# Gate logits of a fused attention, feed-forward and top-1 expert kernel: token columns moving past weights held in four column groups, in place of weights moving past tokens

## The chip, the cores and the metric

The kernel runs on one core of a Trainium2 chip. The metric is the device time of one execution in microseconds (us). Engines are named as in the profile: PE (TensorE, matmul; PEld are its weight loads), DVE (VectorE), ACT (ScalarE), POOL (GpSimd) and SP (SyncE, which issues most DMAs).

## The reference

Three layers run one after another on 1536 tokens (2 batches of 768) of width 512: attention with a local band and a few global keys, a SiLU feed-forward layer of width 2048, and a layer of 8 experts of which each token uses one. The change touches the gates of the last.

```
def _moe2_ref(x, w_gate, w_output_gate, w1, w2):
    logits = x @ w_gate                                  # 1536 x 8
    e_idx = np.argmax(logits, axis=1)
    probs = softmax of logits; gate_w = probs[np.arange(N), e_idx]
    eom = 1.0 / (1.0 + np.exp(-(x @ w_output_gate)))     # 1536 x 8
    for e in range(8):
        mask = e_idx == e
        h = np.maximum(x[mask] @ w1[e], 0.0)             # 512 -> 1024
        out[mask] = gate_w[mask, None] * eom[mask, e, None] * (h @ w2[e])
```

(The two lines on the softmax are shortened here.) The 8 columns of `w_gate` and the 8 of `w_output_gate` stand side by side, so each token needs 16 sums over 512 numbers. An expert must be chosen exactly, so these products are made in float32.

## The kernel before

The tokens are 12 tiles of 128 rows (`n` = 0 to 11), taken in six pairs (`u` = 0 to 5). Attention for the first batch comes first. Then comes the feed-forward stage, a loop over steps `g` (from L966): five groups of pairs, `CH` = [0,1], [2], [3], [4], [5], each with 16 steps `f` over slices of the width 2048. Attention for the second batch is woven into its first four groups.

In each step PE gets, in this order: `s1_mm` (L319, 12 matmuls, x times a slice of `w_in`), two score products of attention where a slot of attention falls in the step (`qkp`, L151), the products with V (`pv`, L224), now and then four transposes (`ms`, L241), then whatever `run_gates` takes from the list `gq`, and last `s2_mm` (L339 to L341, 6 matmuls with `w_out`, of the step two before). On ACT and DVE stand `s1_ev` (tanh on ACT L323, product on DVE L324) and `s1_sp` (ACT L327, DVE L328), which must end before that `s2_mm`'s data two steps later; they are issued ahead of `run_gates` in the same step, so each engine does them first. All engines work through their own instructions strictly in the order written (`manual_schedule`).

The list `gq` sets where the gates go. When a group of pairs is finished, one entry is put on it for each piece of each pair: `s2_ev` (the layer's result to SBUF), two `gate1` (four transposes on PE to a PSUM bank, ACT copies them to `xtf`, so that x stands with its 512 numbers on partitions, 4 blocks of 128), then `gate2`, `gate3`, `gate4`; a step takes one entry from the list, or two at two places that L987 names by number. `gate2` issues `logits` for both tiles and then seven DVE operations (L394 to L400): the maximum, the chosen expert as a one-hot row `eb`, and the running count `esum`. `gate3` begins on PE with six small products `gr` (L406 to L408) that need `eb` and `esum`, and goes on with DVE (L410 to L422) to the row number at which each token is scattered (L429) for its expert. The pair `u`=4 ends one group before the last, so its gates fall into steps of the last group, where no attention is left. The gates of the last pair, `u`=5, are called by hand in `moe2` (L660), between pieces of the first expert's work (`early1`, `late1`).

`logits(n)`, L379, is what the change rewrites: a block of x (128 x 128) is stationary, the 16 columns of `wgs` move, and four such products accumulate to 128 token rows x 16:

```
for k in range(KC): T.matmul(glp[n//2][:,n%2],x[:,k,:],wgs[:,k,:],start=(k==0),stop=(k==KC-1))
```

PSUM banks for these small tiles (`qkp`, `ms`, `gt`, `gl`, `gr`) come from `abank` (L113), which hands out the tags of `atags` in turn; in the stretch where the gates run there are three. A tile that is given a bank waits until everything issued on the tile that had it before has been done.

Of the kernel before, what the change touches and what calls it, by code (L numbers as in the profile page):

```python
# [10 lines left out]
F32 = mybir.dt.float32  # L11
# [5 lines left out]
AF = mybir.ActivationFunctionType  # L17
ALU = mybir.AluOpType
AX = mybir.AxisListType
P = 128  # L20
# [3 lines left out]
def kernel(ctx, tc, qk, v, n_global, n_local, w_in, w_out, wg, w1, w2, out):  # L24
# [38 lines left out]
    vpr=vpr4.bitcast(BF16).rearrange("p z (m d) -> p z m d",m=3)  # L63
    NWI=FB+FB//2
    woh={}
    wgs=const.tile([P,KC,16],F32,name="wgs")
    upper=const.tile([P,P],BF16,name="upper"); ones=const.tile([P,P],BF16,name="ones")
    c3=const.tile([P,8],BF16,name="c3"); rev=const.tile([P,8],F32,name="rev"); tok=const.tile([P,NTT],I32,name="tok")
    esum=const.tile([P,NTT+1,8],BF16,name="esum")
# [43 lines left out]
    def abank(shape,name):  # L113
        tg=atags[0][acnt[0]%len(atags[0])]; acnt[0]+=1
        return ps.tile(shape,F32,tag=tg,name=name,bufs=1)
# [235 lines left out]
    def gate_consts():  # L351
        G.memset(ones,1.0)
        G.memset(upper,1.0)
        G.affine_select(out=upper,in_=upper,pattern=[[1,P]],compare_op=ALU.is_gt,fill=0.0,base=0,channel_multiplier=-1)
        G.memset(esum,0.0)
        G.iota(tok,pattern=[[P,NTT]],base=0,channel_multiplier=1)
        it=mp.tile([P,2,8],I32,tag="gsm",name="it",bufs=2)
        G.iota(it[:,0],pattern=[[-1,8]],base=8,channel_multiplier=0)
        G.tensor_copy(rev,it[:,0])
        G.iota(it[:,1],pattern=[[CAP//P,8]],base=0,channel_multiplier=0)  # L360
        G.tensor_copy(c3,it[:,1])
        for p,w in enumerate(WIN): G.memset(capk[:,p:p+1],8.0*w+8)
        S.dma_start(wgs,wg.rearrange("(k p) e -> p k e",p=P))
    zr=[]
    def rows_init():
        z=mp.tile([P,XW],F32,tag="xT",name="zr",bufs=3); zr.append(z)
# [9 lines left out]
        A.activation(out=x,in_=m,func=AF.Copy)  # L376
    gsm={}
    glp={}
    def logits(n):  # L379
        if n%2==0: glp[n//2]=abank([P,2,16],"gl")  # L380
        x=xts.pop(n)
        for k in range(KC): T.matmul(glp[n//2][:,n%2],x[:,k,:],wgs[:,k,:],start=(k==0),stop=(k==KC-1))  # L382
    def gate2(u):

        for n in (2*u,2*u+1):
            if n in xts: logits(n)
        g=glp.pop(u)
        lg=g[:,:,0:8]
        s=mp.tile([P,2,32],F32,tag="gsm",name="gsm",bufs=2)
        eb=mp.tile([P,2,8],BF16,tag="geb",name="geb",bufs=2)  # L390
        gsm[u]=s,eb
        w=s[:,:,0:8]; mxl=s[:,:,24:25]; mxr=s[:,:,25:26]
        b8=lambda x: x.to_broadcast([P,2,8])
        V.tensor_reduce(out=mxl[:,:,0],in_=lg,axis=AX.X,op=ALU.max)  # L394
        V.tensor_tensor(out=w,in0=lg,in1=b8(mxl),op=ALU.subtract)
        V.scalar_tensor_tensor(out=s[:,:,8:16],in0=w,scalar=0.0,in1=rev[:,None,:].to_broadcast([P,2,8]),op0=ALU.is_equal,op1=ALU.mult)
        V.tensor_reduce(out=mxr[:,:,0],in_=s[:,:,8:16],axis=AX.X,op=ALU.max)
        V.tensor_tensor(out=eb,in0=s[:,:,8:16],in1=b8(mxr),op=ALU.is_equal)
        for t in range(2): V.tensor_tensor(out=esum[:,2*u+t+1],in0=esum[:,2*u+t],in1=eb[:,t],op=ALU.add)
        V.tensor_tensor(out=s[:,:,16:24],in0=g[:,:,8:16],in1=eb,op=ALU.mult)  # L400
# [26 lines left out]
    def gate4(u,t):  # L427
        di,xr=gdi[u]
        G.indirect_dma_start(out=XE[:,:],out_offset=bass.IndirectOffsetOnAxis(ap=di[:,t:t+1],axis=0),in_=xr[:,t,:],in_offset=None,bounds_check=NE*CAP-1,oob_is_err=False)  # L429
# [230 lines left out]
    def moe2():  # L660
        late_split()
        early1(0,0)
        run_gates(2)
        early1(0,1)
        logits(NTT-2)
        early1(1,0)
        run_gates(1)
        late1()
        run_gates(1)
        early1(1,1)  # L670
        run_gates(1)
        early2(0)
        late3()
        order(1)
        moe2_open2()
        load_x(1); load_t(0)
        early3(0,0)
        early2(1)
        early3(0,1); early3(1,0)
        early3(1,1)  # L680
        early4()
        atags[0]=['a','pv','s23']
        LG=2
        steps=[(p,f) for p in range(NE) for f in range(8)]
        for g in range(len(steps)+LG):
            if g<len(steps):
                p,f=steps[g]
                def spl():
                    split_u(4*(p+1)+nq[1]//4,nq[1]%4,nq[1]%4==1); nq[1]+=1
                f1_mm(p,f)  # L690
                if p+1<NE and f==0: nq[:]=[0,0]
                if g==4: flags()
                ns=(0,0,3,3,3,3,2,2)[f] if p+1<NE else 0
                f1_ev(p,f,spl if ns else lambda: None)
                if p+1<NE:
                    for _ in range(ns-1): spl()
                    while nq[0]<min(16,nq[1]+4*(f+1),nq[1]+NQR): load_u(4*(p+1)+nq[0]//4,nq[0]%4); nq[0]+=1
                    if p and f==0: load_x(p+1)
                    if p==0 and f==5:
                        for k,(j,n) in enumerate(tiles(0)): tail(0,j,xwt[0][:,k,0:1],xwt[0][:,k,1:2])  # L700
                    t=tiles(p+1)
                    px=PX
                    if px<=f<px+len(t): prep_x(p+1,t[f-px][0])
            if g>=LG:
                p2,f2=steps[g-LG]
                if p2<NE-1:
                    f2_mm(p2,f2)
                    if f2==7: f2_ev(p2)
                elif f2<LASTF:
                    f2_mm(p2,f2)  # L710
                elif f2==7:
                    for r in tiles(p2):
                        for k in range(LASTF,8): f2_mm(p2,k,[r])
                        f2_ev(p2,[r])
# [225 lines left out]
    with tc.manual_schedule():  # L940
        params()
        want(2); load_v(0)
        table_ints()
        V.tensor_copy(pf,pi)
        table(slice(3,4))
        tab_heads(slice(3,4),slice(3,4),range(H))
        rows_init()
        s=0
        while s<SB:
            for k,e in enumerate(slot_b(s)):  # L950
                e()
                if k==0 and s>=DQ: dec_op()
            if s%2==0 and 4<=s<4+2*NE: rows_clear(s//2-2)
            s+=1
            for x in WP.get(s,()): w_to(*x)
        atags[0]=['s20','s21','s22','s23']
        gate_consts()

        steps=[(c,f) for c in range(len(CH)) for f in range(FB)]
        pend=[]  # L960
        gq=[]
        def run_ev(k):
            for _ in range(min(k,len(pend))): pend.pop(0)()
        def run_gates(k):
            for _ in range(min(k,len(gq))): gq.pop(0)()
        for g in range(len(steps)+LAG):  # L966
            live=g<len(steps)
            if live:
                c,f=steps[g]
                if c==0:  # L970
                    w_to(0,0,g+LI); w_to(0,1,g+(LO if g<LS else 1)); w_to(2,0,f+1)
                for u in CH[c]: s1_mm(u,f)
                for u in CH[c]: s1_ev(u,f)
                if c==0:
                    for _ in range(2):
                        if s<SB+4: pend+=slot_b(s); s+=1
                    if g==3: atags[0]=['a']
                    if f==FB-1: s=SB
                elif c<4 and s<NS+4 and (f>1 and f!=8 if c==1 else f%2==0):
                    pend+=slot(s); s+=1  # L980
                run_ev(2 if c==0 else 1)
                for u in CH[c]: s1_sp(u,f)
                run_ev(4 if c==0 else 3 if c==1 else 3 if f%2 else 0)
                if g<=FB:
                    w_to(1,0,g+2); w_to(2,1,g-1); w_to(1,1,g)
                if g==FB: load_v(SB//4)
                if g>=LAG+FB: run_gates(2 if g-(len(CH)-1)*FB in (2,4) else 1)  # L987
            if g>=LAG:
                c2,f2=steps[g-LAG]
                s2_mm(c2,f2)  # L990
                if f2==FB-1:
                    for u in CH[c2]: gq.append(lambda u=u: s2_ev(u))
                    if c2==0: gq.append(lambda: atags.__setitem__(0,['a','s22','s23']))
                    for u in CH[c2]:
                        for n in (2*u,2*u+1): gq.append(lambda n=n: gate1(n))
                        for fn in (gate2,gate3,lambda u: gate4(u,1)): gq.append(lambda u=u,fn=fn: fn(u))
                    run_gates(3 if c2==0 else 1)
                    if c2==len(CH)-2: gq.append(lambda: order(0))
                    if c2==len(CH)-2: gq.append(moe2_open)
            if live and c>0:  # L1000
                if f==0: load_wol(c,0); load_wol(c,1)
                if f+2<FB: load_wol(c,f+2)
            if g>=len(steps)-FB: moe2_pre(g-len(steps)+FB)
        moe2()
# [43 lines left out]
```

## Time and profile before

| | us |
|---|---|
| median of 3 runs | 621.5 |
| lowest and highest | 619.34 and 621.65 |
| the profiled execution | 621.69 |
| its span, first to last instruction | 620.0 |
| PE busy (4054 matmuls) | 590.6, 95% |
| PE weight loads busy | 500.6, 81% |
| DVE busy | 389.1, 63% |
| ACT busy | 303.0, 49% |
| POOL busy | 186.2, 30% |

The profiled execution is 0.2 above the median of the runs, and 1.7 of it lie outside the span. A busy PE in this table is one that has at least one matmul in flight; matmuls overlap, so what a group of them costs is read from the start of its first to the start of the next group, not from durations. A float32 matmul shows as two records, so the eight matmuls of a pair's logits are 16.

### The profile page before, as it was taken

Reading aid. Unit: us, or ns where it says so; the run is one execution under the profiler, and the core shown is the slowest. Engines: PE = TensorE matmul, PEld = TensorE weight load, DVE = VectorE, ACT = ScalarE, POOL = GpSimd, SP = SyncE. Lnnn points to the kernel's source line nnn. Section 1 sums busy time; section 2 is a strip of 40 time slices with the busy share of each in tenths; the row PEclk is TensorE's granted clock in tenths of the full one; section 3 lists DMA queues with packets and bytes.
Section 4 is the critical chain, followed back from the end, with each engine's and each line's share of the span. In section 5 each row is a group of like instructions: output and inputs, shape, how many; then the busy total and the mean of one; then the engine's idle time right before and its main releaser. Section 6 shows DMA issues by size and latency. Waiting matters only on the chain.

```text
span 620.0 us, 12009 instructions
## 1 busy us (share of the span) xinstructions
PE 590.6 (95%) x4054; PEld 500.6 (81%) x4054; DVE 389.1 (63%) x1069; ACT 303.0 (49%) x802; POOL 186.2 (30%) x233
## 2 busy tenths in 40 slices
PE   2999899999999999999999999999899999999996
PEld 1566788888888888888889999888788888888884
DVE  4388669999737764756463345744844678778840
ACT  5377634334353445343532234644653666776641
POOL 3367614444314252131221001112231432331321
PEclk9999999999999999999999999999999999999999
DMA  7639725674355587465444327607845378569500
GB/s 255 243 79 355 218 89 159 215 221 158 116 160 148 149 192 170 106 177 130 115 89 141 86 84 259 254 19 246 263 162 185 127 259 269 184 212 290 162 17 21
DMA packets 81511, 105.18 MB, mean 170 GB/s; under 512 B 29978, under 2 KB 44314, under 8 KB 81441
## 3 DMA queue, kind: packets, MB, share of 16 engines
q1 hardware_dynamic: 75712, 94.79, 50.4%
q0 software_dynamic: 2288, 6.39, 2.8%
q10 hardware_dynamic: 3440, 3.15, 1.6%
q8 instruction: 34, 0.56, 0.4%
q14 instruction: 37, 0.30, 0.2%
HBM read 81.46 MB, written 17.99 MB: 160 GB/s over the span
## 4 chain that ended last, share of the span: by engine, by line
PE 69%; issue 8%; DVE 8%; DMA 6%; ACT 4%; POOL 3%; SPq 1%; ACTq 0%; POOLq 0%; DVEq 0%
PE s L319 17%; PE s L339 6%; PE s L340 5%; PE s L341 5%; PE h L616 5%; PE h L622 4%; PE qkp L151 4%; PE y L639 4%; PE y L641 4%; PE y L640 4%; PE tp L194 3%; PE h L617 2%; POOL wol L303 2%; PE pv L224 2%; PE gl L382 1%
## 5 line engine op out<-in xcount | busy, mean ns | idle before, releaser
L319 PEld LDWEIGHTS s<-xT,wi 128*128 128x128 f32 x1152 | 147.3, 190 | 13.1 <-DVE g L328 6.0
L319 PE MATMUL s<-xT,wi 128*128 128x256 f32 x1152 | 152.2, 284 | 1.9 <-DVE xT L248 1.4
L323 ACT ACTIVATE u<-s 128x256 f32<-128x256 f32 x96 | 35.3, 381 | 112.3 <-PE s L319 111.5
L324 DVE SCALAR_TENSOR_TENSOR s<-u,s 128x256 f32<-128x256 f32 x96 | 39.8, 427 | 79.4 <-ACT u L323 79.4
L339 PE MATMUL s<-woh,g 128*128 128x512 f32 x192 | 79.2, 413 | 0.0
L491 DVE TENSOR_TENSOR uq<-qr,uq 128x512 fp32r<-128x512 f32 x87 | 71.2, 841 | 7.2 <-ACT uq L490 4.4
L340 PE MATMUL s<-woh,g 128*128 128x512 f32 x192 | 75.5, 393 | 0.0
L490 ACT ACTIVATE uq<-qr 128x512 fp32r<-128x512 f32 x112 | 66.4, 626 | 4.4 <-DMA qr<-in_w_dram 4.1
L328 DVE TENSOR_TENSOR g<-s,g 128x256 fp32r<-128x256 f32 x96 | 39.3, 422 | 31.7 <-ACT g L327 27.3
L327 ACT ACTIVATE g<-s 128x256 fp32r<-128x256 f32 x96 | 35.7, 380 | 40.3 <-DVE s L324 40.3
L639 PE MATMUL y<-uq,hh 128*128 128x512 f32 (+6 forms) x136 | 55.2, 406 | 0.0
L641 PE MATMUL y<-uq,hh 128*128 128x512 f32 (+6 forms) x136 | 53.6, 394 | 0.0
L640 PE MATMUL y<-uq,hh 128*128 128x512 f32 (+6 forms) x136 | 53.4, 393 | 0.0
L491 POOL TENSOR_TENSOR uq<-qr,uq 128x512 fp32r<-128x512 f32 x25 | 32.9, 1326 | 62.1 <-ACT uq L490 62.1
L151 PE MATMUL qkp<-ring 64*128 64x256 f32 (+1 forms) x192 | 36.0, 455 | 14.3 <-DMA ring<-in_qk_dram 13.4
L170 ACT ACTIVATE t<-t,mx 128x256 f32<-128x256 f32 (+1 forms) x96 | 45.8, 480 | 6.5 <-DVE mx L163 4.6
L631 ACT ACTIVATE hh<-h 128x224 fp32r<-128x224 f32 (+6 forms) x64 | 23.3, 364 | 47.3 <-DVE h L629 27.3
L632 DVE SCALAR_TENSOR_TENSOR hh<-h,hh 128x224 fp32r<-128x224 f32 (+6 forms) x64 | 25.3, 395 | 31.8 <-ACT hh L631 31.8
L339 PEld LDWEIGHTS s<-woh,g 128*128 128x128 f32 x192 | 36.3, 189 | 7.1 <-ACT u L323 2.0
L340 PEld LDWEIGHTS s<-woh,g 128*128 128x128 f32 x192 | 36.3, 189 | 5.0
L577 POOL DMA_INDIRECT out_dram<-y,ixt x17 | 17.4, 1024 | 74.9 <-ACT y L646 56.7
L341 PE MATMUL s<-wolr,g 128*128 128x512 f32 x128 | 39.6, 390 | 0.0
(215 smaller groups left out, 1071.7 us busy)
## 6 DMA issues: line engine op xcount, KB each, us to landing
qr<-in_w_dram SPq DMA_DIRECT2D x128, 256.0 KB
wolr<-wlo_d SPq DMA_DIRECT2D x64, 256.0 KB
wiraw<-in_w_in_dram SPq DMA_DIRECT2D x16, 512.0 KB
wraw<-in_w_out_dram SPq DMA_DIRECT2D x13, 512.0 KB
xe<-zr SPq DMA_DIRECT2D x8, 792.0 KB
wlo_d<-wol SPq DMA_DIRECT2D x16, 256.0 KB
xw<-xe SPq DMA_DIRECT2D x15, 264.0 KB
ring<-in_qk_dram SPq DMA_DIRECT2D x12, 256.0 KB
```

The lines of the kernel that those rows point to most:

```text
L151: T.matmul(q[:,sl],w[:,z,1],w[:,z:z+1,0] if i==0 else w[:,0:3:2,0] if z==0 else w[:,z-1:z+1,0],start=True,stop=True)
L170: A.activation(out=t[:,j,:ce],in_=t[:,j,:ce],func=AF.Exp,scale=0.125,bias=mx[n][:,h:h+1],accum_out=ss[n][:,h:h+1])
L319: T.matmul(t,w[:,ww,kc,:],x[:,xx,kc,:],start=(k==0),stop=(k==11)); k+=1
L324: V.scalar_tensor_tensor(out=t,in0=u,scalar=1.0,in1=t,op0=ALU.add,op1=ALU.mult)
L339: T.matmul(o,g[u][:,0,sl],wh,start=(f==0),stop=False)
L340: T.matmul(o,g[u][:,1,sl],wh,start=False,stop=False)
L341: else: T.matmul(o,g[u][:,0,sl],wl,start=False,stop=(f==FB-1))
L490: A.activation(out=t[:,0],in_=r,func=AF.Copy)
L491: (G if (i%2 if pool is None else pool) else V).tensor_tensor(out=t[:,1],in0=r,in1=t[:,0],op=ALU.subtract)
L639: T.matmul(o,g[:,0,sl],w[:,0],start=(f==0),stop=False)
L640: T.matmul(o,g[:,1,sl],w[:,0],start=False,stop=False)
L641: T.matmul(o,g[:,0,sl],w[:,1],start=False,stop=(f==7))
```

## The change

`logits` is turned round. The 16 weight columns of a block (with the 16 of the next block behind them, so that a group is 32 wide) are now stationary, in column group `k` for block `k`, and the 128 tokens of the block move. The four products don't accumulate: each writes its own 32 partitions of a tile of 128 x 128, of which ACT makes a copy in SBUF (in the place of x's first block). A second product has that copy stationary and a constant `sel` (128 x 16, ones where the row is 32k + column) moving; it adds the four groups and brings tokens back to partitions. This second product stands at the head of `gate2`; the first ones get an entry of their own in the list, `gate2a`, ahead of it. The entry makes the list longer, and a third step (number 5 after the last group's start) takes two entries. In `moe2` both tiles' first products stand together ahead of `early1(1,0)`, and the second behind it. The bank of `gl` now holds a tile from `gate2a` to the end of `gate2`'s DVE operations.

```
-    wgs=const.tile([P,KC,16],F32,name="wgs")
+    wgs=const.tile([P,KC+1,16],F32,name="wgs"); sel=const.tile([P,16],F32,name="sel")
...
-        S.dma_start(wgs,wg.rearrange("(k p) e -> p k e",p=P))
+        S.dma_start(wgs[:,0:KC],wg.rearrange("(k p) e -> p k e",p=P))
+        G.memset(wgs[:,KC],0.0)
+        G.tensor_tensor(out=sel,in0=ident[:,0:16],in1=ident[:,32:48],op=ALU.add)
+        for k in (2,3): G.tensor_tensor(out=sel,in0=sel,in1=ident[:,32*k:32*k+16],op=ALU.add)
...
     def logits(n):
-        if n%2==0: glp[n//2]=abank([P,2,16],"gl")
-        x=xts.pop(n)
-        for k in range(KC): T.matmul(glp[n//2][:,n%2],x[:,k,:],wgs[:,k,:],start=(k==0),stop=(k==KC-1))
-    def gate2(u):
-
+        if n%2==0: glp[n//2]=abank([P,KC,P],"gl")
+        x=xts.pop(n); q=glp[n//2][:,1+n%2]
+        for k in range(KC): T.matmul(q[32*k:32*(k+1),:],wgs[:,k:k+2,:].rearrange("p a e -> p (a e)"),x[:,k,:],start=True,stop=True)
+        A.activation(out=x[:,0,:],in_=q,func=AF.Copy); xls[n]=x
+    def gate2a(u):
         for n in (2*u,2*u+1):
             if n in xts: logits(n)
-        g=glp.pop(u)
+    def gate2(u):
+
+        g=glp.pop(u)[:,0,0:32].rearrange("p (t e) -> p t e",t=2)
+        for t in range(2): T.matmul(g[:,t],xls.pop(2*u+t)[:,0,:],sel,start=True,stop=True)
...
         logits(NTT-2)
+        run_gates(1)
         early1(1,0)
...
-                if g>=LAG+FB: run_gates(2 if g-(len(CH)-1)*FB in (2,4) else 1)
+                if g>=LAG+FB: run_gates(2 if g-(len(CH)-1)*FB in (2,4,5) else 1)
...
-                        for fn in (gate2,gate3,lambda u: gate4(u,1)): gq.append(lambda u=u,fn=fn: fn(u))
+                        for fn in (gate2a,gate2,gate3,lambda u: gate4(u,1)): gq.append(lambda u=u,fn=fn: fn(u))
```

What this moves is seen in the order of the instructions. First PE in the steps 3 and 4 of the last group, where the gates of pair `u`=4 stand; `s` are tiles of the feed-forward layer (12 matmuls of `s1_mm`, 6 of `s2_mm`), `gl` the logits, `gr` the products of `gate3`. Before:

```order
L319 MATMUL s_4580<-xT,wi 128x256 x12
L382 MATMUL gl<-wgs,xtf 128x16 x8
L339 MATMUL s_4570<-woh,g 128x512
L340 MATMUL s_4570<-woh,g 128x512
L339 MATMUL s_4571<-woh,g 128x512
L340 MATMUL s_4571<-woh,g 128x512
L341 MATMUL s_4570<-wolr,g 128x512
L341 MATMUL s_4571<-wolr,g 128x512
L319 MATMUL s_4626<-xT,wi 128x256 x12
L406 LDWEIGHTS upper
L406 MATMUL gr<-geb,upper 128x8
```

Now:

```order
L319 MATMUL s_4601<-xT,wi 128x256 x12
L386 MATMUL gl<-xtf,wgs 32x128 x8
L339 MATMUL s_4591<-woh,g 128x512
L340 MATMUL s_4591<-woh,g 128x512
L339 MATMUL s_4592<-woh,g 128x512
L340 MATMUL s_4592<-woh,g 128x512
L341 MATMUL s_4591<-wolr,g 128x512
L341 MATMUL s_4592<-wolr,g 128x512
L319 MATMUL s_4639<-xT,wi 128x256 x12
L394 MATMUL gl<-sel,xtf 128x16 x2
L413 LDWEIGHTS upper
L413 MATMUL gr<-geb,upper 128x8
```

The logits' last product has come to stand directly ahead of `gr`; between the two there was a whole `s2_mm` and a whole `s1_mm`.

DVE at the same place, before:

```order
L324 SCALAR_TENSOR_TENSOR s_4580<-u,s_4580 128x256
L328 TENSOR_TENSOR g<-s_4580,g 128x256
L394 TENSOR_REDUCE gsm<-gl 128x2
L395 TENSOR_TENSOR gsm<-gl,gsm 128x2x8
L396 SCALAR_TENSOR_TENSOR gsm<-gsm,rev 128x2x8
L397 TENSOR_REDUCE gsm<-gsm 128x2
L398 TENSOR_TENSOR geb<-gsm 128x16
L399 TENSOR_TENSOR esum<-esum,geb 128x8 x2
L400 TENSOR_TENSOR gsm<-gl,geb 128x2x8
L324 SCALAR_TENSOR_TENSOR s_4626<-u,s_4626 128x256
L328 TENSOR_TENSOR g<-s_4626,g 128x256
L410 TENSOR_TENSOR gsm<-gr,geb 128x2x8
```

Now:

```order
L324 SCALAR_TENSOR_TENSOR s_4639<-u,s_4639 128x256
L328 TENSOR_TENSOR g<-s_4639,g 128x256
L401 TENSOR_REDUCE gsm<-gl 128x2
L402 TENSOR_TENSOR gsm<-gl,gsm 128x2x8
L403 SCALAR_TENSOR_TENSOR gsm<-gsm,rev 128x2x8
L404 TENSOR_REDUCE gsm<-gsm 128x2
L405 TENSOR_TENSOR geb<-gsm 128x16
L406 TENSOR_TENSOR esum<-esum,geb 128x8 x2
L407 TENSOR_TENSOR gsm<-gl,geb 128x2x8
L417 TENSOR_TENSOR gsm<-gr,geb 128x2x8
```

`gate2`'s seven operations stand behind `L324` and `L328` of the later step, the one in which PE reaches `gr`.

Last PE for the last pair, in `moe2`; `eh` is the first expert's early product, `ec` the gather of its rows. Before:

```order
L555 MATMUL eh<-qb,exT 128x512 x6
L382 MATMUL gl<-wgs,xtf 128x16 x4
L555 MATMUL eh<-uq,exT 128x512 x6
L382 MATMUL gl<-wgs,xtf 128x16 x4
L536 MATMUL ec_5176<-eI,ehl 128x128 x2
```

Now:

```order
L562 MATMUL eh<-qb,exT 128x512 x6
L386 MATMUL gl<-xtf,wgs 32x128 x8
L562 MATMUL eh<-uq,exT 128x512 x6
L394 MATMUL gl<-sel,xtf 128x16 x2
L543 MATMUL ec_5205<-eI,ehl 128x128 x2
```

The second tile's first products have moved ahead of the six `eh`, and the small product took their place ahead of `ec`.

## Rows read from the trace of the kernel before

**Rows 1.** Busy time by stretch: start:end, length, busy by engine (instructions), clock, DMA

```profile
184.00:403.00 219.00, 218.01 (x1779) 191.36 (x1778) 123.43 (x410) 92.52 (x272) 47.02 (x48) 1.00 0.56 149
425.00:590.00 165.00, 161.23 (x906) 136.74 (x906) 115.88 (x236) 103.43 (x233) 49.29 (x41) 1.00 0.66 217
```

**Rows 2.** Timeline of PE at the first pair's logits: start, length, instruction

```profile
184.51 1.96 PE L382 MATMUL gl<-wgs,xtf 128*128 128x16 f32 x16
186.31 0.48 PE L339 MATMUL s<-woh,g 128*128 128x512 f32 x1
```

**Rows 3.** Timeline at the last pair's second logits and what follows

```profile
407.55 0.60 ACT L558 ACTIVATE ehs<-eh 128x512 f32<-128x512 f32 x1 [0.75 <-PE eh L555]
408.16 1.64 PE L555 MATMUL eh<-uq,exT 128*128 128x512 f32 x6
409.63 0.96 PE L382 MATMUL gl<-wgs,xtf 128*128 128x16 f32 x8
410.44 1.97 PE L536 MATMUL ec<-eI,ehl 128*128 128x128 f32 x16
410.63 0.18 DVE L394 TENSOR_REDUCE gsm<-gl 128x2 f32<-128x16 f32 x1 [3.47 <-PE gl L382]
412.25 0.18 PE L406 MATMUL gr<-geb,upper 128*128 128x8 bf16 x1
```

**Rows 4.** Timeline of PE in attention: products in two column groups, what follows

```profile
61.20 0.66 PE L209 MATMUL px<-pT,vpr 128*64 128x128 f32 x8
61.79 0.70 PE L151 MATMUL qkp<-ring 64*128 64x256 f32 x4
```

**Rows 5.** The same eight, looked at through two narrow windows, 61.66:61.70 and 61.75:61.76

```profile
61.47 0.39 PE L209 MATMUL px<-pT,vpr 128*64 128x128 f32 x4
...
61.58 0.28 PE L209 MATMUL px<-pT,vpr 128*64 128x128 f32 x2
```

**Rows 6.** Instructions of line L209: durations min/median/max in ns, the weight loads

```profile
L209 PEld LDWEIGHTS px<-pT,vpr x176: 132/137/231, 21.3 to 83.6; 128*64 128x64 f32 x176
```

**Rows 7.** Timeline of pair u=4: DVE of gate2, then the step of gate3

```profile
364.71 0.42 DVE L328 TENSOR_TENSOR g<-s,g 128x256 fp32r<-128x256 f32 x1 [0.45 <-ACT g L327]
365.05 0.17 DVE L394 TENSOR_REDUCE gsm<-gl 128x2 f32<-128x16 f32 x1
366.10 0.36 DVE L399 TENSOR_TENSOR esum<-esum,geb 128x8 bf16<-128x8 bf16 x2
366.37 0.17 DVE L400 TENSOR_TENSOR gsm<-gl,geb 128x16 f32<-128x16 f32 x1
367.77 0.18 PE L406 MATMUL gr<-geb,upper 128*128 128x8 bf16 x1
367.93 0.47 PE L339 MATMUL s<-woh,g 128*128 128x512 f32 x1
368.02 0.39 ACT L323 ACTIVATE u<-s 128x256 f32<-128x256 f32 x1 [3.35 <-PE s L319]
369.32 0.42 DVE L328 TENSOR_TENSOR g<-s,g 128x256 fp32r<-128x256 f32 x1 [0.45 <-ACT g L327]
```

**Rows 8.** Timeline of pair u=2: gr, DVE of gate3, the next step's scores

```profile
259.04 0.17 PE L406 MATMUL gr<-geb,upper 128*128 128x8 bf16 x1 [0.26 <-DVE mx L160]
261.38 0.16 DVE L410 TENSOR_TENSOR gsm<-gr,geb 128x16 f32<-128x16 f32 x1
262.18 0.70 PE L151 MATMUL qkp<-ring 64*128 64x256 f32 x4
```

**Rows 9.** Timeline behind gate3 of pair u=1: DVE's last, the next step's scores

```profile
218.43 0.20 DVE L230 RECIPROCAL rs<-rs 128x8 f32<-128x8 f32 x1
219.40 0.30 PEld L151 LDWEIGHTS qkp<-ring 64*128 64x128 f32 x4
```

**Rows 10.** Busy time by stretch at the end, columns as in rows 1

```profile
610.00:615.00 5.00, 3.90 (x17) 2.02 (x15) 0.00 (x0) 1.17 (x2) 1.10 (x2) 1.00 0.17 55
615.00:620.00 5.00, 0.00 (x0) 0.00 (x0) 0.00 (x0) 0.00 (x0) 0.82 (x1) 0.89 0.02 5
```

More of the change, by code (lines that the diff above doesn't have):

```diff
@@ L378 @@
     glp={}
+    xls={}
     def logits(n):
-        if n%2==0: glp[n//2]=abank([P,2,16],"gl")
-        x=xts.pop(n)
-        for k in range(KC): T.matmul(glp[n//2][:,n%2],x[:,k,:],wgs[:,k,:],start=(k==0),stop=(k==KC-1))
-    def gate2(u):
+        if n%2==0: glp[n//2]=abank([P,KC,P],"gl")
[3 more added lines that the diff above has]
+    def gate2a(u):
         for n in (2*u,2*u+1):
             if n in xts: logits(n)
-        g=glp.pop(u)
+    def gate2(u):
+        g=glp.pop(u)[:,0,0:32].rearrange("p (t e) -> p t e",t=2)
+        for t in range(2): T.matmul(g[:,t],xls.pop(2*u+t)[:,0,:],sel,start=True,stop=True)
         lg=g[:,:,0:8]
```

## The prediction, written before the changed kernel ran

> **What bounds the kernel now.** I read the busy time by stretch first. From 184 to 403, where the first five pairs' gates lie, PE is busy for 218.01 of 219.00 us, and in the experts' stage for 161.23 of 165.00 [rows 1]. DVE and ACT stay far below. So PE is the bound on both sides of every place that the change touches, and there a microsecond of PE work saved, or of PE standing still, moves the end by about a microsecond. Then I looked at what the logits cost: not the durations, which overlap, but the start of the group and the start of the next one. At the first pair that is 184.51 to 186.31, 1.80 us for 16 records [rows 2]. Last I followed, for each place of the new order, what PE would wait for there.
>
> **What is removed.** Five pairs at 1.80 make 9.0. At the last pair the two tiles stand apart, 409.63 to 410.44 for one [rows 3], 0.81, so 1.62 for both. Together 10.6 us of PE.
>
> **What is added on PE: the first products.** No row of this trace has four column groups. The nearest is attention's product with V, which writes two halves of the partitions from 64 stationary columns each, with 128 columns moving, as the new logits have. Eight records of it take from 61.20 to 61.79 [rows 4]. Through narrow windows one sees that they start two by two: four are in flight from 61.47 on, the last two from 61.58 [rows 5]. So a round of two costs 0.11, four rounds 0.44, and 0.15 of the 0.59 goes to the change of division, 0.10 of it on leaving (61.58 to 61.79 is a round and 0.10). If all four groups run together, a pair's 16 records are four rounds too, and cost the same 0.59. At three pairs (u=1, 4, 5) full-width work stands directly ahead, where a score product, itself divided, stood or nothing had to change; I add 0.10 each. Sum 6 x 0.59 + 0.3 = 3.8. The bounds: if nothing ran side by side, 16 rounds of 0.11 and the same 0.15, 1.9 a pair; at best four rounds without any price of changing, 0.44. I take the middle value because the row it comes from has the same moving width, the same type and the same change of division.
>
> The same rows bear on a rule that speaks against this change. Two rounds 0.11 apart leave no room for a weight load of 0.137 [rows 5, 6] between them, so loads of one column half run while the other half's product is in flight. The Trainium skill (page "TensorE: Matmul & The Clock Gate", Part 3 on packing small matmuls) says that a weight load overlaps with matmuls in flight only where the row group differs, which column groups don't give; by that a round would be a load and a product. What that would cost is a rival below, and two column halves in this trace don't show it.
>
> **The second product.** Two matmuls, 4 records with a 128-wide stationary side and 16 columns moving, just the form that is removed; at 1.80/16 = 0.11 a record that is 0.45 a pair, 2.7 for six. Added on PE in all 6.5; PE's own work falls by 10.6 - 6.5 = 4.1 us.
>
> **What is added elsewhere.** Twelve ACT copies of 128 x 128. In the steps the second product comes a whole step later, so they are covered. At the last pair the cover is the six `eh` between: ACT is done with `ehs` at 407.55 + 0.60 = 408.15 [rows 3], and the six `eh` there took from 408.16 to 409.63. They now begin a little earlier, about 408.0, and the second product at about 409.3; even at 0.5 each, two copies would be done by then. If that cover were gone, PE would wait for at most those two copies, 1 us. Four small POOL operations at the start stand among other constants, before anything that waits; I cost them at nothing.
>
> **The wait that the change adds.** The third doubled step puts `gate2` and `gate3` of pair u=4 into one step. PE meets the second product and, directly behind, `gr`, which needs `eb` and `esum` from the DVE operations that the second product feeds; and those stand behind `L324` and `L328` of the same step. By the rows: `gr` stood at 367.77 and was over at 367.93; ACT's tanh of that step begins at 368.02 and DVE's `L328` at 369.32 [rows 7]. In the step before, from the start of `L328` at 364.71 to the first of the two additions to `esum` (the pair is 366.10 plus 0.36, so half at 366.28) it is 1.57. So `gr` can't end before 369.32 + 1.57 = 370.9. With only the second product ahead of it it would have ended at 367.93 + 0.45 = 368.4. PE stands still for about **2.6 us**, and `s2_mm` of the step is queued behind. Nothing else can run on PE then, since it works in order, and PE is the bound. What was ahead of `gr` before, a whole `s2_mm` and `s1_mm`, was its cover.
>
> **Bank waits.** The logits' bank is held a step longer, until `L400` (now at the end of the later step's DVE work) has read it, while score products take the three banks in turn. Of pair u=2 the second score product of the step after gets that bank. `gate2` now begins on DVE where `gate3` did, at 261.38 [rows 8], and takes 365.05 to 366.37 + 0.17, 1.49 [rows 7], so the bank is free at 262.9. The scores stood at 262.18; they come 0.45 later for the second product, and 0.16 and 0.26 earlier because `gr` and its wait of 0.26 have left that place [rows 8]: 262.2. A wait of 0.7. At u=1 DVE is free at 218.63 [rows 9], so 220.1 against 219.40 + 0.45 = 219.85: 0.25. At u=0 the same reading gives none, and at u=3 no scores follow in the next step. On the other side the wait of 0.26 at `gr` goes at u=2 and its twin at u=3: 0.5.
>
> **The last pair.** 1.62 goes and 0.69 + 0.45 comes, already in the sum. `L394` would start some 0.5 earlier than 410.63; `gr` waits behind `ec` as before (410.44 to 412.25 against a DVE chain of about 1.5 from 410.63 [rows 3]), so no new wait.
>
> **The sum.** 621.69 - 4.1 + 2.6 + 0.7 + 0.25 - 0.5 = 620.6 for an execution like the profiled one; the median of the runs lies 0.2 under that one, so 620.4 (the rivals below are worked out on the profiled execution). That is 0.2% under 621.5: less than the 0.5% (3.1 us: 618.4 and 624.6) that a measurement of this kernel can tell from no change. What the new products save is given back at one place where two steps of a chain were put together.
>
> **Rivals.**
> - *Two at a time.* If only two column groups run side by side, as the trace shows, a pair needs eight rounds: 4 x 0.11 x 6 = 2.6 more, 623.1. For it: rows 4 show two. Against: nothing in them shows that two is the most. If every round instead had a load of 0.137 ahead of its product, four rounds cost 4 x 0.137 more, 3.3 for six pairs: 623.8. Against that, rows 5. By the rule of the page named above it would be this second figure. Together 0.16; 0.06 of it for the load.
> - *One after another, slower.* If the four products of a tile run one by one, so that the change does not do what its column groups are for, each pair pays 12 more rounds of 0.11, 1.3, at the same place in each step: 7.9, so 628.4. The change comes out slower than before once a pair pays 0.2 more than I take, and by over 0.5% from 0.7. Rows 4 and 5 speak against it. 0.07.
> - *The clock.* PE's clock is 1.00 up to 615 and falls only when PE has long stopped, 0.89 in the last stretch with PE at 0 [rows 10]. If the wait at u=4 took it down to the lower of its two levels, each us there would cost half a us; it takes some 8 us of it to be slower by over 0.5%. 0.03.
> - *The waits are covered, faster.* If `gr`'s wait at u=4 cost nothing, because the step's own chain on ACT and DVE starts sooner than I read or PE catches up later, 617.9. Nothing in rows 1 leaves PE room to catch up. 0.10, with smaller gains elsewhere in it.
>
> **How the numbers follow.** My forecast has 0.64. Its own range is 618.6 to 622.2: the first products at best (1.2 less), of the bank waits (0.9 less if they vanish, 0.9 more if they double), of the wait at u=4 (2.2 to 3.0), beside a spread of the runs that alone is 2.3. The range for 8 in 10 goes on to 623.8, which takes in the first rival. Faster by over 0.5%: 0.12, from the last rival and the low end of the forecast. Slower: 0.13, from one by one, the clock and the upper end of two at a time. Within: 0.75.
>
> **What would show it.** PE from the first record of the new `gl` to the next group: 0.6 to 0.7 for 16 records, where 1.0 would mean two at a time and 1.9 one by one; the records starting in fours. PE idle ahead of `gr` at u=4 for 2.6 us, put down to DVE. Score products at u=2 idle some 0.7 for DVE. `gr` no more waiting at u=2 and 3. PE busy over the whole span some 4 lower, its idle time some 3 higher. If the logits are cheap and the wait at u=4 is not there, I have misread the order; if the wait is there and the time falls by 4 all the same, PE was not the bound that rows 1 make it.

## The result, and the profile after

The changed kernel takes 626.14 us (median of five runs, 624.4 to 628.14) beside 621.13 for the kernel before (five runs). The ratio is 1.0088, with a 95% interval of 1.0061 to 1.0116: slower by 0.9%, outside the range of the prediction. Beside the later experiments it gave 626.41 where before gave 619.26, a ratio of 1.0099 (1.0067 to 1.0132).

The profiled execution took 628.14, and its span is 626.4 with a mean granted clock of 0.990, where before had 0.999. Part 1 of its page, first line (busy us, share of the span, instructions), and then the two stretches of [rows 1] again, columns as there:

```profile
PE 587.5 (94%) x4078; PEld 495.2 (79%) x4078; DVE 386.9 (62%) x1069; ACT 306.2 (49%) x814; POOL 186.8 (30%) x237
```

```profile
184.00:403.00 219.00, 211.16 (x1735) 182.61 (x1735) 115.19 (x392) 87.67 (x263) 42.75 (x45) 0.98 0.54 145
425.00:590.00 165.00, 161.64 (x908) 137.19 (x907) 110.64 (x230) 100.52 (x223) 49.94 (x41) 1.00 0.63 215
```

The experts' stage is as it was (161.23 of 165 before, 161.64 now). In the gates' stretch PE is idle for 7.8 us where it had been idle for 1.0, and the clock there is 0.98; the first pair's first products, at 180.6 to 182.9, now lie ahead of it. PE's busy time over the whole span fell by 3.1 us (590.6 to 587.5); since work at a lower clock counts as longer busy time, this sum alone prices no term.

What PE waits for, from 160 to 432 (line waited at, who ended the wait: us in total, times, longest):

```profile
PE gl L386 <- ACT xtf L387: 5.6, 6, 1.5
PE gr L413 <- DVE geb L405: 2.4, 1, 2.4
PE qkp L151 <- DVE gsm L407: 1.1, 2, 0.8
```

The second line is the wait that the prediction has at 2.6, the third the two bank waits that it has at 0.95 together. The first line is in none of its terms. It is six waits, one a pair, and twice as large as the one that was foreseen.

The first pair shows where it comes from. The timeline of `after` (start, length, engine, line; in brackets the idle time before and who ended it), PE and ACT:

```profile
180.37 0.38 ACT L323 ACTIVATE u<-s 128x256 f32<-128x256 f32 x1 [1.39 <-PE s L319]
...
180.63 0.43 PE L386 MATMUL gl<-xtf,wgs 128*32 128x128 f32 x8
180.65 0.39 ACT L170 ACTIVATE t<-t,mx 128x128 f32<-128x128 f32 x1
...
181.42 0.62 ACT L133 ACTIVATE vpr<-vraw 128x512 bf16<-128x512 f32 x1
...
181.94 0.36 ACT L327 ACTIVATE g<-s 128x256 fp32r<-128x256 f32 x1
...
182.21 0.27 ACT L387 ACTIVATE xtf<-gl 128x128 f32<-128x128 f32 x1
...
182.53 0.43 PE L386 MATMUL gl<-xtf,wgs 128*32 128x128 f32 x8 [1.47 <-ACT xtf L387]
...
182.88 0.50 PE L339 MATMUL s<-woh,g 128*128 128x512 f32 x1
```

The eight records of the first tile are over at 181.06. Those of the second begin at 182.53, just after ACT has finished the copy of the first tile (182.21 + 0.27 = 182.48). That copy is short, but it stands behind everything that the step had already given ACT: `L323`, `L170`, `L133`, `L327`. The order of the program's instructions on PE has the wait written out. Each piece is the place of the first pair; "waits" is the engine whose progress is awaited. In `after`:

```
491 L386 MATMUL gl<-xtf,wgs 32x128 [waits Activation_49]
492 L386 MATMUL gl<-xtf,wgs 32x128 x3
493 L386 MATMUL gl<-xtf,wgs 32x128 [waits Activation_49]
494 L386 MATMUL gl<-xtf,wgs 32x128 x3
```

The first wait is for `xtf` itself, which before had too. The second is new: `logits(n)` issues four products and then the copy, and `gate2a` calls it twice. Both tiles lie in one PSUM tile, in one bank, so the second tile's products are ordered behind ACT's reading of the first. The Trainium skill (page "PSUM — Partial Sum Buffer", section "PSUM bank collisions raise a hardware error") gives the reason for such an order: two engines must not be in the same bank and partitions at once, even at other columns. No run here shows a collision; what the trace shows is the order, 182.53 behind 182.48.

At the other five pairs the same wait is 0.50, 0.96, 0.96, 1.22 and 0.50.

The clock has a part of its own. Busy time by stretch in `after` (columns as in [rows 1], the clock third from the end), around the first pair and around the `gr` of pair u=4:

```profile
180.00:183.50 3.50, 2.03 (x26) 1.22 (x25) 1.96 (x9) 2.38 (x9) 1.16 (x1) 1.00 0.36 63
183.50:187.00 3.50, 3.50 (x15) 3.12 (x14) 0.00 (x0) 0.00 (x0) 0.67 (x1) 0.51 0.42 101
187.00:191.00 4.00, 4.00 (x36) 3.48 (x36) 2.51 (x12) 1.42 (x6) 0.67 (x1) 1.00 0.34 118
...
371.20:378.10 6.90, 6.17 (x26) 5.42 (x27) 2.33 (x15) 0.78 (x3) 1.16 (x2) 0.51 0.25 75
```

Behind the wait of 1.47, and again from the last 0.7 us of the wait of 2.4 at `gr` (which lasted until 371.93), PE runs at the lower of its two levels (0.5, that is 1.2 GHz), though it is busy without a pause for nearly all of the two stretches. 3.5 and 6.9 us at 0.51 do the work of half their length, so about 5 us are lost in this execution, 0.3 of them while PE stood in that wait anyway. The prediction gave this 0.03.

### The profile page after: what moved, and what is told of

The parts are those of the page before. It is cut to its first block, busy times and chain, and to the rows that moved or that the text cites. A ratio compares the mean times of both kernels' runs of the same rounds, so it can differ in the third digit from the quotient of the medians.

```text
span 626.4 us, 12086 instructions
## 1 busy us (share of the span) xinstructions
PE 587.5 (94%) x4078; PEld 495.2 (79%) x4078; DVE 386.9 (62%) x1069; ACT 306.2 (49%) x814; POOL 186.8 (30%) x237
## 4 chain that ended last, share of the span: by engine, by line
PE 63%; DVE 12%; issue 8%; DMA 7%; ACT 6%; POOL 3%; SPq 0%; POOLq 0%; DVEq 0%; ACTq 0%
PE s L319 16%; PE s L339 6%; PE s L340 5%; PE s L341 5%; PE h L623 4%; PE h L629 4%; PE y L646 4%; PE y L648 3%; PE y L647 3%; DMA ring<-in_qk_dram 3%; PE qkp L151 3%; PE tp L194 2%; PE h L624 2%; POOL wol L303 2%; PE pv L224 2%
## 5 line engine op out<-in xcount | busy, mean ns | idle before, releaser
L319 PEld LDWEIGHTS s<-xT,wi 128*128 128x128 f32 x1152 | 149.4, 193 | 13.4 <-DVE g L328 6.0
L319 PE MATMUL s<-xT,wi 128*128 128x256 f32 x1152 | 154.1, 286 | 1.9 <-DVE xT L248 1.4
L324 DVE SCALAR_TENSOR_TENSOR s<-u,s 128x256 f32<-128x256 f32 x96 | 39.7, 426 | 92.2 <-ACT u L323 92.2
L323 ACT ACTIVATE u<-s 128x256 f32<-128x256 f32 x96 | 35.2, 381 | 117.5 <-PE s L319 112.7
L339 PE MATMUL s<-woh,g 128*128 128x512 f32 x192 | 80.4, 419 | 0.0
L498 DVE TENSOR_TENSOR uq<-qr,uq 128x512 fp32r<-128x512 f32 x87 | 74.7, 882 | 7.0 <-ACT uq L497 4.0
L340 PE MATMUL s<-woh,g 128*128 128x512 f32 x192 | 76.3, 397 | 0.0
L328 DVE TENSOR_TENSOR g<-s,g 128x256 fp32r<-128x256 f32 x96 | 39.3, 422 | 30.3 <-ACT g L327 27.1
L327 ACT ACTIVATE g<-s 128x256 fp32r<-128x256 f32 x96 | 35.7, 380 | 39.4 <-DVE s L324 38.9
L170 ACT ACTIVATE t<-t,mx 128x256 f32<-128x256 f32 (+1 forms) x96 | 45.8, 480 | 4.6 <-DVE mx L163 3.8
```

Source lines behind the costliest of these rows:

```text
L170: A.activation(out=t[:,j,:ce],in_=t[:,j,:ce],func=AF.Exp,scale=0.125,bias=mx[n][:,h:h+1],accum_out=ss[n][:,h:h+1])
L319: T.matmul(t,w[:,ww,kc,:],x[:,xx,kc,:],start=(k==0),stop=(k==11)); k+=1
L324: V.scalar_tensor_tensor(out=t,in0=u,scalar=1.0,in1=t,op0=ALU.add,op1=ALU.mult)
L339: T.matmul(o,g[u][:,0,sl],wh,start=(f==0),stop=False)
L340: T.matmul(o,g[u][:,1,sl],wh,start=False,stop=False)
L498: (G if (i%2 if pool is None else pool) else V).tensor_tensor(out=t[:,1],in0=r,in1=t[:,0],op=ALU.subtract)
```

## The experiments

Theory M: the six waits for the copies are the loss, together with the wait at `gr` and the clock that falls behind such waits; the new products themselves cost what was forecast. Its main rival: the products with the array in four column groups cost more than they seem to. R1, R2 and R3 are what the text written ahead of each run calls its rivals; they are not the same in all.

**copies_last: both tiles' products ahead of both copies.**

```
     def logits(n):
...
-        A.activation(out=x[:,0,:],in_=q,func=AF.Copy); xls[n]=x
+        xls[n]=x
     def gate2a(u):
         for n in (2*u,2*u+1):
             if n in xts: logits(n)
+        for t in range(2): A.activation(out=xls[2*u+t][:,0,:],in_=glp[u][:,1+t],func=AF.Copy)
```

> The changed kernel with one thing moved: both tiles' first products are issued before the two ACT copies, so that the second tile's products no longer stand behind the copy of the first. The wait at gr of pair u=4 stays. Theory M (the loss is made of three parts: about 5.6 us at the second tile's products, 2.4 us at gr, and 1 to 5 us in which the clock falls behind these waits): 626.1 - 5.6 and a part of the clock's, 618.5 to 620.5; no PE idle ahead of L386, PE still idle some 2.4 us ahead of gr. Rival R1 (the wait at gr is the cost, and the clock's fall behind it; the second tile's waits lie beside other work): 625 to 626, since gr's wait is untouched.

Measured: 620.18 beside 620.37 of before on the same chip (ratio 0.9998, 0.9974 to 1.0022). On PE the first pair's products are now one group with one wait:

```
491 L386 MATMUL gl<-xtf,wgs 32x128 [waits Activation_49]
492 L386 MATMUL gl<-xtf,wgs 32x128 x7
```

Its waits from 160 to 422, the two largest:

```profile
PE gr L414 <- DVE geb L406: 2.4, 1, 2.4
PE qkp L151 <- DVE gsm L408: 1.0, 2, 0.8
```

The line with `xtf` is gone, and with it 5 to 6 us of time. The wait at `gr` is untouched, so this text's R1 falls; and since the products are still in four column groups, so does the main rival. What is left is the forecast's own balance: the saving, less the `gr` wait and the bank waits and some clock (0.9956 on average against 0.9980, at most 1.5 us), comes out at no change.

**gate3_later: `gate3` of u=4 a step after `gate2`, copies as in after.**

```
-                if g>=LAG+FB: run_gates(2 if g-(len(CH)-1)*FB in (2,4,5) else 1)
+                if g>=LAG+FB: run_gates({2:2,5:3}.get(g-(len(CH)-1)*FB,1))
```

> The changed kernel with gate3 of pair u=4 one step later (the doubled entries at number 4 go, step 5 takes three: gate3, gate4 and order), so that a whole s2_mm and s1_mm stand again between the second product and gr. The six waits at the second tile stay. Theory M: 626.1 - 2.4 and the clock's fall behind that wait, up to 3.4: 621 to 624, PE idle ahead of L386 some 5.6 in all, none ahead of gr. Rival R1: back to about 618 to 620, since the wait that costs is gone.

Measured: 627.31, ratio 1.0099 (1.0066 to 1.0132). This is a miss: M had 621 to 624, its R1 618 to 620, and there is no gain over after. Its waits on PE from 160 to 430, the first two, then a wait of the SP queue from 370 to 410:

```profile
PE gl L386 <- ACT xtf L387: 5.6, 6, 1.5
PE s L341 <- DMA wolr<-wlo_d: 1.8, 1, 1.8
```

```profile
SPq L506 <- DMA xe<-xr,gdi: 4.0, 1, 4.0
```

The `gr` wait is gone, and a wait of 1.8 for `wolr` has come, the weights of the feed-forward layer's last product. `gate3` ends in the scatter of the pair's rows; a step later, the scatter lands later; the first expert's load (`L506`) stands on SP's queue and needs the scattered rows, so SP holds for 4.0 us, and the loads of `wolr` are queued behind it on SP. The DMA engines are full there too (share 1.04 in the row below), but so they are in before (1.05 from 386 to 394), without such a wait. And the clock: in the profile's rows of the stretch behind that wait,

```profile
396.60:400.00 3.40, 3.40 (x16) 3.25 (x15) 1.80 (x4) 2.17 (x5) 0.00 (x0) 0.53 1.04 391
```

it is again at the lower level. So 2.4 and a fall were exchanged for 1.8 and a fall.

**both: the two edits together.**

> Both edits: copies behind both tiles' products, and gate3 of u=4 a step later. Theory M: all waits but those of the banks are gone, the clock doesn't fall between 100 and 600 us, and what the turned products save on PE is left: 621.1 - 4.1 and about 0.5 either way, 616.5 to 618. Rival R1: the same as gate3_later alone. Rival R2 (the turned products themselves cost more than the trace shows, by the changes of division or the clock): no better than before, 620 to 623.

Measured: 618.71, ratio 0.9970 (0.9948 to 0.9993). Faster than before by 0.3%, so its R1 and R2 fall. It is 0.7 us above what M expected, which had no wait for `wolr` in it; that wait is there as in gate3_later:

```profile
PE s L341 <- DMA wolr<-wlo_d: 1.5, 1, 1.5
PE qkp L151 <- DVE gsm L408: 1.0, 2, 0.8
```

**before_joined: the kernel before, with `gate2` and `gate3` of u=4 in one step.**

```
-                if g>=LAG+FB: run_gates(2 if g-(len(CH)-1)*FB in (2,4) else 1)
+                if g>=LAG+FB: run_gates(2 if g-(len(CH)-1)*FB in (2,3) else 1)
```

> The kernel before, with one number changed: gate2 and gate3 of pair u=4 in one step, so that gr stands directly behind the old logits and must wait for the DVE chain. Nothing of the new products is in it. By the rows of before gl ends at 364.83 and the first addition to esum at 366.28, so a wait of about 1.5. Theory M: 621.1 + 1.5 = 622.6, and up to 1.7 more in runs where the clock falls behind it. If PE has room to catch up: 621.

Measured: 621.5, ratio 1.0037 (1.0009 to 1.0064). The wait is there, at half the size it has in after, since the old logits on PE take longer than the small product (1.85 us against 0.52, from the first start to the last end) and so cover more of the chain on DVE:

```profile
PE gr L406 <- DVE geb L398: 1.1, 1, 1.1
```

The median is 1.1 us above that of before. The mean is 2.1 above it, and its executions had a granted clock of 0.9965 on average against 0.9980, which over 620 us is 0.9: 1.1 of wait and 0.9 of clock. So the step put together costs its wait and a little clock, and the greater part of what after lost is not in it.

**before_wait: the kernel before, and nothing of the change but the wait.** After each tile's old products ACT copies the tile's 16 logits to a place that nothing reads.

```
         for k in range(KC): T.matmul(glp[n//2][:,n%2],x[:,k,:],wgs[:,k,:],start=(k==0),stop=(k==KC-1))
+        A.activation(out=x[:,0,0:16],in_=glp[n//2][:,n%2],func=AF.Copy)
```

> The kernel before, with its own products, and one thing added: after each tile's four logit products ACT copies the tile's 16 logits out of PSUM (into a stretch of xtf that nothing reads any more), so that the second tile's products stand behind that copy, as in the changed kernel. Nothing of the column groups is in it. Theory M (the wait for the copy is the loss, the new products are not): six waits of 0.4 to 1.5 us at the second tile's first product, 5 to 5.6 us together, and 625 to 628 us where before measures 620.4. Rival R1 (the products with the array in four column groups cost what was lost): 620 to 621.5, as before. Rival R3 (a wait costs only in sum, as the clock falls behind it in some executions): 625 and up, with the granted clock under 1.00 behind at least one of the waits in the profile.

Measured: 625.38 beside 619.26, ratio 1.0112 (1.0076 to 1.0148). A copy between the tiles, without any column groups, is enough to lose as much as the change lost, though not in the same parts. The waits are smaller than M expected: not 5 but

```profile
PE gl L382 <- ACT xtf L383: 2.6, 5, 0.7
```

because the old products keep PE busy longer while ACT gets to the copy. The old products, now in two parts, also take 0.9 more in all (11.4 us for 10.5 in before, each group from its start to the start of the next, less idle time). Most of the rest is the clock, as R3 had it. The first pair, PE's timeline and then the clock by stretch:

```profile
183.38 1.07 PE L382 MATMUL gl<-wgs,xtf 128*128 128x16 f32 x8
185.19 1.07 PE L382 MATMUL gl<-wgs,xtf 128*128 128x16 f32 x8 [0.74 <-ACT xtf L383]
```

```profile
183.00:187.00 4.00, 3.26 (x25) 2.91 (x25) 2.11 (x11) 2.19 (x9) 1.83 (x2) 0.99 0.44 98
187.00:190.40 3.40, 3.40 (x15) 3.12 (x14) 0.91 (x6) 0.00 (x0) 0.00 (x0) 0.51 0.33 89
```

Here the clock fell behind a wait of only 0.74 us, with narrow products (16 columns) on either side of it. Over its six executions the mean granted clock was 0.987 to 0.995, 0.9912 on average, where the 22 of before on that chip had 0.997 to 0.999, 0.9983 on average. A clock lower by 0.0071 over some 620 us is at most 4.4 us; with 2.6 of waits and the 0.9 that makes 7.9, and the mean times differ by 7.0 (626.4 and 619.5). So the clock's part is some 3.5 to 4.4 us here, more than the waits. For after, measured beside it, the clock was 0.9962 on average: 1.3 us.

**mid: a better order for u=4.** copies_last, with the list at its old pace, and one entry more taken behind `s2_mm` in the step of `gate1`, so that the first products stand there and everything after them in the steps of before.

```
-                if g>=LAG+FB: run_gates(2 if g-(len(CH)-1)*FB in (2,4,5) else 1)
+                if g>=LAG+FB: run_gates(2 if g-(len(CH)-1)*FB in (2,4) else 1)
...
                 s2_mm(c2,f2)
+                if g==(len(CH)-1)*FB+2: run_gates(1)
```

> Both tiles' first products ahead of both copies, and for the pair u=4 the first products one place earlier, behind the second-layer products of the step that transposes the pair, so that second product, rank products, scatter and order stand in the steps in which they stood before. Theory M: no wait for a copy between the tiles, no wait of 2.4 at gr, and no wait of 1.5 to 1.8 for wolr, since the scatter no longer holds up SP's queue; what is left is the saving on PE of about 4 us, less 0.5 to 1.5 for the waits for xtf and for the bank: 616.5 to 618.0 beside 620.4 of before. Rival (every wait that goes is taken up by the next late thing, as the wolr wait took up the gr wait): 618 to 620, as the version with both repairs.

Measured: 617.23 beside 619.26, ratio 0.9965 (0.9946 to 0.9985). It is the fastest version here, 0.35% faster than before. From 160 to 425 these are the waits over 0.5 that are left:

```profile
PE qkp L151 <- DVE gsm L408: 1.0, 2, 0.8
PE h L624 <- DVE hh L640: 0.6, 1, 0.6
```

The second is in the experts' stage, and before has it too. No `xtf`, no `gr`, no `wolr`. It does not beat "both" by anything the ratios can tell (0.9965 and 0.9970), though between the two profiled executions the stretch with all the gates (table below) is shorter by 3.3 us. Its gain of 2.0 us is 0.4 less than the least that was expected.

**mid_between: the same order for u=4, copies between the tiles as in after.**

> The order of the version above for u=4, but each tile's copy right behind its products, as in the changed kernel. Theory M: the changed kernel less its gr wait of 2.4 us and less what the clock lost behind it, and without the wolr wait that took its place a step later: 621.5 to 624 where the changed kernel measures 626. Rival (the wait at gr costs nothing, since something else is late anyway): 625.5 to 626.5.

Measured: 621.68, ratio 1.0039 (1.0018 to 1.0059).

```profile
PE gl L386 <- ACT xtf L387: 4.9, 6, 1.5
```

After less this version is 4.7 us: 2.4 for the `gr` wait, 0.7 less waiting at `gl`, and 0.6 for the clock (0.9972 on average, after 0.9962), with 1.0 left over. So the `gr` wait does cost its length, once nothing takes its place. And mid_between less mid, 4.4 us (6.0 by the stretch in the table below), is the copies between the tiles alone.

**after_again: the changed kernel beside these.**

> The changed kernel as it is, beside the others on the same chip: 625 to 627 us by every theory, about 1.009 of before. In its profile theory M expects 5.6 us of waits at the second tile's first products again and 2.4 us at gr; where the granted clock falls to 0.5 it is right behind one of the longer of these waits, though not always behind the same.

Measured: 626.41 (623.3 to 629.94), ratio 1.0099. Its waits are the same to the tenth:

```profile
PE gl L386 <- ACT xtf L387: 5.6, 6, 1.5
...
PE gr L413 <- DVE geb L405: 2.4, 1, 2.4
```

This time the clock fell once, behind the first pair's wait, and not at `gr` (a wait of 2.37 that ended at 375.18); by stretch, PE alone:

```profile
185.00:192.00 7.00, 6.21 (x45) 0.76 0.52 140
...
371.00:382.00 11.00, 8.63 (x64) 1.00 0.27 93
```

So the waits are fixed by the program and the falls are not.

**All versions against one another.** The start of an execution varies (the first feed-forward product of after began at 68.42 in one profile and at 71.67 in the other, behind the same work), which blurs single spans. From the start of the first `L319` record to the start of the experts' first product (`L616` in before) it is out of the way. The length of that stretch in the profiled executions, less before's 350.16; the waits that differ; the time lost to the clock there (half of what was spent at the lower level); and the median less that of before beside it:

| | waits at the second tile | at `gr` u=4 | `wolr` | clock | stretch | median |
|---|---|---|---|---|---|---|
| after | 5.6 | 2.4 | | 5.1 | +10.9 | +5.0 |
| after_again | 5.6 | 2.4 | | 1.7 | +8.6 | +7.2 |
| gate3_later | 5.6 | | 1.8 | 1.7 | +7.7 | +6.9 |
| mid_between | 4.9 | | | 0 | +3.5 | +2.4 |
| copies_last | | 2.4 | | 1.7 | +1.3 | -0.2 |
| both | | | 1.5 | 0 | +0.8 | -1.7 |
| mid | | | | 0 | -2.5 | -2.0 |
| before_wait | 2.6 | | | 1.7 | +4.6 | +6.1 |
| before_joined | | 1.1 | | 0 | +0.8 | +1.1 |

Take after_again, with each group read from its start to the start of the next, less idle time. The old products take 10.5 us in before; the new ones take 4.7 and the second products 2.5, so 3.3 are saved. Waits add 8.0, and 1.0 for the bank, less the 0.5 that `gr` no longer waits at u=2 and u=3; the clock adds 1.7, and score products take 0.7 more, which hangs on the bank wait at u=2 (below). That is 7.6 of 8.6. In mid the first products, in one part, take 3.4 and the second ones 2.4, so 4.8 are saved, and the same sum gives -3.6 where -2.5 stands. The microsecond that is left is the same in both; in mid 0.9 of it is spread in small pieces over the feed-forward products.

## Why the prediction was wrong, point by point

- **The step that failed** is one sentence under "What is added elsewhere": "In the steps the second product comes a whole step later, so they are covered." It asked who needs a copy's result, the second product, and found cover. It did not ask what is queued behind the copy, in the bank that it reads: the second tile's first products. In after PE waits 5.6 us there, and after against copies_last and mid_between against mid show that the copies' place alone is worth 4.4 to 6 us. The order of instructions, read with its waits, showed this before anything ran: a group of eight products that had been one piece stood there as two, the second with a wait on ACT. And a price could have been bounded from [rows 7], as it was for `gr`: what a step's gates give to ACT and DVE stands behind that step's own `L323` to `L328`, which were still to come when PE was through.
- The rule that bore on it was passed over. The Trainium skill (page "TensorEngine Tiling (Array Packing)", section "PSUM Bottleneck") says that tiling speeds up TensorE but not the evacuation of PSUM, which may become the bottleneck. The trace agrees in kind, with 0.43 us of products ahead of 1.47 of waiting for a copy of 0.27; but what made it a bottleneck was the copy's place in the queue, not its length.
- **The first products were right where they stand in one part.** Forecast 0.59 for a pair and 0.10 more at three. In mid, PE's timeline at pair u=1, the new products and then the next group, then the second product of u=2 and the next group:

```profile
206.97 0.65 PE L386 MATMUL gl<-xtf,wgs 128*32 128x128 f32 x16
207.54 0.50 PE L339 MATMUL s<-woh,g 128*128 128x512 f32 x1
...
254.39 0.52 PE L395 MATMUL gl<-sel,xtf 128*128 128x16 f32 x4
254.75 0.49 PE L339 MATMUL s<-woh,g 128*128 128x512 f32 x1
```

  0.57 for 16 records, and so at all six pairs: the 0.10 more at three did not show. The second product takes 0.36 (0.45 at u=0 and u=1, as forecast). Together 4.8 us are saved in mid where 4.1 were forecast. In after the copy parts the products, and a pair takes 0.43 + 0.35 = 0.78 besides its wait: 4.7 for six pairs where the forecast had 3.8.
- **Four at a time was right.** In after, narrow windows over the first tile's eight records (start:end, length, PE and PEld busy, clock), `L386` alone:

```profile
180.62:180.65 0.03, 0.02 (x4) 0.02 (x4) 1.00 0.00 0
180.65:180.76 0.11, 0.11 (x4) 0.11 (x8) 1.00 0.00 0
180.76:180.79 0.03, 0.03 (x8) 0.02 (x4) 1.00 0.00 0
```

  Four records and four loads have started within 0.03 us, and the next four start together 0.13 later. So the rivals "two at a time" and "one after another" fall. The Trainium skill (page "TensorE: Matmul & The Clock Gate", Part 3, the list of what overlaps) lets a weight load overlap with products in flight only where the row group differs. The trace does not agree, and the rival of 623.8 falls with it: the groups share all their rows, and yet the second four's loads, of 0.106 to 0.110 us each, run while only the first four's products are in flight (the second row above); a pair's 16 loads one after another would be 1.7 us, and the whole group takes 0.57.
- **The wait at `gr` was right in place and size**, 2.4 against 2.6 (its own rows give 370.9 - 368.4 = 2.5, and the rivals are worked out on a sum of 620.5; nothing hangs on this 0.1). In its worth it was right only where nothing takes its place (4.7 us from after to mid_between, with 0.7 of that at `gl`); gate3_later shows the other case.
- **The bank waits**: 0.7 at u=2 and 0.25 at u=1 were forecast. At u=1 PE waits for 0.79, ahead of all four score records of the step. At u=2 it waits for 0.27 only, but between the second and the third, so that two score products that had run side by side in before now run one after the other. In after:

```profile
261.87 0.70 PE L151 MATMUL qkp<-ring 64*128 64x256 f32 x2
262.83 0.67 PE L151 MATMUL qkp<-ring 64*128 64x256 f32 x2 [0.27 <-DVE gsm L407]
263.43 0.18 PE L413 MATMUL gr<-geb,upper 128*128 128x8 bf16 x1
```

  From the first score record to the next group it is 1.56, where before has 0.63 (262.18 to 262.81). So u=2 costs 0.93, and the two together 1.7 where 0.95 were forecast. `gr` no longer waits at u=2 and u=3, as forecast.
- **The last pair**: "no new wait" was wrong in the same way as the main step, by 0.50 at its second tile.
- **The clock** had 0.03, on the grounds that PE's clock fell only at the very end [rows 10], when PE had long stopped. That argued from a trace with no such wait in it: before has nothing over 0.5 us from 160 to 425. In after it fell at waits of 1.5 and 2.4. It is the smaller part of the loss in after (5.1 us in the profiled execution, 1.3 on average in the later ones) and the larger in before_wait.
- "PE has no room to catch up" held: each wait came through to the end at about its length, or at more.

The forecast's sum mended: 620.6, and 5.6 for the copies' waits, 0.9 for the first products in two parts, 0.8 at the score products and 4.8 for the clock (5.1 less the 0.3 that lay in a wait), less 0.4 for a `gr` wait and second products that came out smaller, make 632.3. The profiled execution of after was through with the opening 3.8 us sooner than that of before (68.42 against 72.26 at the first `L319`), which leaves 628.5. It took 628.14.

## What to carry to other kernels

For each added instruction that reads a PSUM tile, ask two things: who needs what it writes, and who next writes the bank that it reads; on a tile that two groups of products share, put all the products ahead of the first copy. A short instruction waits for its whole queue, so price a wait on it by what its engine has been given before it in that step, not by its own length. And when a wait is removed, follow the DMAs that move with it: here a scatter a step later held SP's queue, and the weights behind it took the wait over.

## What the runs showed of the hardware that was not expected

- The granted clock fell to 0.5 for 3.4 us (once 6.8) at single waits of PE of 0.74, 1.47, 1.8 and 2.4 us, in executions where PE was otherwise busy. The low level began between 0.7 us before the wait's end (at `gr` in after) and 1.7 us after it (in before_wait), and lay almost wholly on PE's work, not on its standing still. The same wait did not do it every time: 1.47 at the first pair did in after and after_again and not in gate3_later and mid_between, 2.4 at `gr` did in after and copies_last and not in after_again, 1.5 for `wolr` did not in "both", 1.1 did not in before_joined, and the 1.4 to 1.6 for `xT` ahead of the feed-forward stage did not in any profile.
- Four float32 products in four column groups, each with 128 rows, start within 0.03 us of one another, and eight records with their eight loads take 0.43 us, 0.35 of it until the next group starts. Changing the array's division is in that figure: in mid the four rounds of a pair start at 206.97, 207.10, 207.21 and 207.32 and the next group at 207.54, so a round is 0.11 to 0.13 and some 0.1 is for the change on leaving.
